# A token-mixing kernel on one core: single row blocks in 64-row halves, one chunk's sums moved, and one step's weight turns re-ordered

## The chip, the cores and the metric

The kernel runs on one NeuronCore of a Trainium2 chip. The time is device microseconds of one execution, the median of several runs. TensorE (PE in the profile) multiplies, VectorE (DVE) and ScalarE (ACT) do elementwise work, GpSimd (POOL) adds and issues DMAs, SyncE (SP) issues DMAs.

## What is computed

Batch 8, sequence 4224, width 192, in two stages. The first is a causal softmax-weighted convolution with 7 taps and one set of weights for each of 8 heads. The second mixes tokens with two dense 4224x4224 matrices:

```python
theta = x @ w_theta
zr, zi = x * np.cos(theta), x * np.sin(theta)
y = np.einsum('ts,bsd->btd', w_tok_r, zr) + np.einsum('ts,bsd->btd', w_tok_i, zi)
u = x + y
out = u + np.maximum(u @ w_ch, 0.0)
```

The two products with 4224x4224 matrices are nearly all of the work.

## The kernel before, in words

**Chunks and blocks.** The tokens that are summed over are cut into 33 chunks of 128 (`NK`), in three groups of 11 (`NW`). The tokens that are written are cut into 33 row blocks of 128 (`NT`), in 17 units: 16 pairs and one single block, the 33rd. The 8 x 192 columns are 1536, seen as two halves of the width (h = 0, 1) of 768 each; a product has 384 moving columns (`BH`), so 768 columns are two products (q = 0, 1).

**Steps.** `Step` t takes one unit (`unit(t)`) and the chunks active at t (`active(t)`; a group's chunks come in over six steps, base 0 to 5, and each stays for 17 steps). There are 58 steps, in order, in rounds of 17: steps 0 to 16 start each unit (`first`), 17 to 40 add to it, 41 to 57 finish it (`final`). The single block has steps 6, 23, 40 and 57, with 11, 11, 9 and 2 chunks. The sums of a unit (`pv`, f32 in SBUF) are loaded from and stored to DRAM (`part`) between rounds.

**Pairs in seven products.** A pair step is a 2x2 product for each chunk: two row blocks (from the two matrices, names "11", "12", "21", "22"; the second digit is the matrix) by two halves of the width (Z11, Z12, Z21, Z22 and differences of them, T1 to T4). It is done in Winograd's form, 7 products in place of 8, with four sums of weights: S1 = 21 + 22, S2 = S1 - 11, S3 = 11 - 21, S4 = 12 - S2. The order of the runs (`runs`, L513) is 11, S1, S2, S4, S3, 12, 22, each over all chunks, with two products (q) a chunk: 154 products in a step of 11 chunks. Each accumulates in a PSUM tile `y` (`ypool`, 2 buffers of two banks): c1 has the runs 11, S2, S3 and 22, c2 S1 and S4, c3 the run 12 in the buffer that c2 leaves. After a run the tile is copied (ScalarE, L496) or added (DVE, L498) into `pv`, and the next run on the same tile waits for that. A single block takes plain products: 4 runs, 88 products of 128x384 with 11 chunks.

**Weights.** `load_w` (L391) loads one matrix's rows for a step as four DMAs from POOL's queue into `st`, of which there are two buffers; a pair has a load of matrix r (m = 1) and one of matrix i (m = 2). `turn` (L404) transposes them 32x32-wise on DVE into a weight tile `wt`, for a pair four turns ("11" and "21" read the first load, "22" and "12" the second), and `wsum` (L416) forms S1 to S4 on DVE. A load can start once the buffer's last turn is done.

**Order.** Each engine's order is written out by hand: `in_order` ties every DVE, PE, ACT and POOL instruction to the one before it. In a step, `mix` issues products and, between them, the events of `step_events(t)`, each with a place from 0 to 7 in units of a seventh of the step. Among the events are the next step's turns and sums (`w_tasks`), the loads for the step after it, and the work on new chunks: convolution (`conv`, L228: 16 products with 96 rows, 64 columns, the two 64-row halves of a PSUM tile in turn), transposes (L174), theta (L150), sine (L303), products (L309) and the differences T1 to T4 (`sums`, L318). The same is done in the front loop (L908) for the first 11 chunks, where a list `LATER` (chunks 8, 9 and 10) has its sums moved into steps 3 and 4. From round 2 on, x is added to `pv` on POOL (`add_x`, L476), with one load buffer `xr` from SP's queue; `paced` ties it to DVE's last instruction at that place.

```python
    LATER = [k for k in range(NW) if start[k] == start[NW - 1]]
    LATER = [LATER[0] - 1] + LATER
```

Of the kernel before, what the change touches and what calls it, by code (L numbers as in the profile page):

```python
# [10 lines left out]
ALU = mybir.AluOpType  # L11
# [5 lines left out]
def kernel(  # L17
# [67 lines left out]
    def pe(ins):  # L85
        return in_order("pe", ins)

    def dve(ins):
        return in_order("dve", ins)
# [261 lines left out]
    class Step:  # L351


        def __init__(self, t):
            self.t, self.u, self.ks = t, unit(t), active(t)
            self.n = len(self.ks)
            self.tbs = [tb for tb in (2 * self.u, 2 * self.u + 1) if tb < NT]
            self.pair = len(self.tbs) == 2
            self.first = t < NU
            self.final = t + NU >= NSTEP  # L360
            self.late = self.final and self.n < NW
            visits = [v for v in range(NU, NSTEP) if v % NU == t % NU]
# [12 lines left out]
            self.plain = self.first and self.pair and self.n <= NP  # L375
            self.time = 0.324 * self.n * (8 if self.plain else 7 if self.pair else 5 if self.n <= 2 else 4)
            self.closing = False
            self.st, self.w, self.xr, self.ub, self.uT, self.pv = {}, {}, {}, {}, {}, []

# [4 lines left out]
        def load_w(self, m):  # L384

            w = (moe_w_tok_r, moe_w_tok_i)[m - 1]
            st = wpool.tile([P, 2, NQ, NW * Q], F16, name="st", tag="st", bufs=2)
            n, nb = self.n * Q, len(self.tbs)
            for a in range(NQ):
                t0 = token(self.ks[0], a)  # L390
                pool(nc.gpsimd.dma_start(  # L391
                    out=st[a * Q : (a + 1) * Q, 0:nb, :, 0:n]
                    .rearrange("i r bt s -> i (r bt) s"),
                    in_=w[self.tbs[0] * P : (self.tbs[0] + nb) * P, t0 : t0 + n]
                    .rearrange("(bt i) s -> i bt s", i=Q),
                ))
            self.st[m] = st
# [4 lines left out]
        def turn(self, name):  # L402
            self.w[name] = self.wtile()
            dve(nc.vector.transpose(  # L404
                self.w[name][:, 0 : self.n, :, :],
                self.st[int(name[1])][:, int(name[0]) - 1, :, 0 : self.n * Q]
                .rearrange("p bt (c j) -> p c bt j", j=Q),
            ))

        def wsum(self, name):  # L410
            a, b, op = {
                "S1": ("21", "22", ALU.add), "S2": ("S1", "11", ALU.subtract),
                "S3": ("11", "21", ALU.subtract), "S4": ("12", "S2", ALU.subtract),
            }[name]
            self.w[name] = self.wtile()
            dve(nc.vector.tensor_tensor(  # L416
                out=self.w[name][:, 0 : self.n, :, :],
                in0=self.w[a][:, 0 : self.n, :, :],
                in1=self.w[b][:, 0 : self.n, :, :], op=op,
            ))  # L420

        def w_tasks(self):

            if not self.pair:
                return [(0.25, lambda: self.turn("11")), (4.2, lambda: self.turn("12"))]
            if self.plain:
                return []
            if self.ahead_of_single():
                return [
                    (0.3, lambda: self.turn("22")), (1.1, lambda: self.wsum("S1")),  # L430
                    (1.9, lambda: self.wsum("S2")), (2.9, lambda: self.turn("12")),
                    (4.0, lambda: self.wsum("S4")),
                ]
            return [
                (0.25, lambda: self.turn("11")), (1.2, lambda: self.turn("21")),
                (2.05, lambda: self.wsum("S3")), (2.2, lambda: self.turn("22")),
                (3.05, lambda: self.wsum("S1")), (3.3, lambda: self.wsum("S2")),
                (4.2, lambda: self.turn("12")), (5.1, lambda: self.wsum("S4")),
            ]

        def ahead_of_single(self):
            return self.final and not steps[self.t - 1].pair and self.pair

        def early_tasks(self):

            return [
                (5.9, lambda: self.turn("11")), (7.0, lambda: self.turn("21")),
                (7.01, lambda: self.wsum("S3")),
            ]
# [110 lines left out]
        def mix_halves(self, events):  # L560
# [31 lines left out]
            for _, f in events:  # L592
                f()

        def mix(self, events):

            if self.n <= 2 and not self.first:
                yield from self.mix_halves(events)
                return
            items = list(self.products())  # L600
            events = sorted(events, key=lambda e: e[0])
            y = {}
            for j, (wn, zn, cn, c, opens, closes, to) in enumerate(items):
                if opens:
                    y[cn] = ypool.tile([P, 2, PC], F32, name="y", tag="y")
                while events and events[0][0] * len(items) <= 7 * j:
                    events.pop(0)[1]()
                k = self.ks[c]
                yield k
                for q in range(2):  # L610
                    pe(nc.tensor.matmul(  # L611
                        y[cn][:, q, 0:BH],
                        lhsT=self.w[wn][:, c, :, :].rearrange("p bt i -> p (bt i)"),
                        rhs=chunks[k].z[:, zn, q * BH : (q + 1) * BH],
                        start=opens, stop=closes,
                        skip_group_check=True,
                    ))
                if to:
                    self.give(y[cn], *to)
            for _, f in events:  # L620
                f()
            if not self.final:
                for i, tb in enumerate(self.tbs):
                    nc.sync.dma_start(
                        out=part[(self.t // NU) % 2][tb, :, :], in_=self.pv[i]
                    )

        def cast_half(self, i, h, gs, by_dve):

# [85 lines left out]
    steps[-2].closing = True  # L715
    NPS = max(s.t for s in steps if s.plain)
    LATER = [k for k in range(NW) if start[k] == start[NW - 1]]
    LATER = [LATER[0] - 1] + LATER
    EARLY = max(k for k in range(NK) if start[k] <= NPS)
    outputs = [  # L720
        (sum(s.time for s in steps[: t + 1]) + at, f)
# [5 lines left out]
    def step_events(t):  # L727
        found = []
        s = steps[t]
        if t + 1 < NSTEP:  # L730
            found += steps[t + 1].w_tasks()
            if not steps[t].ahead_of_single():
                found.append((1.6, steps[t + 1].load_rows))
            for i in steps[t + 1].adds:
                if (t + 1, i) != first_add:
                    found.append((2 + 2 * i, lambda i=i: steps[t + 1].load_x(i)))
                found.append((3.6 + 2 * i, lambda i=i: steps[t + 1].add_x(i)))
        here = [(r, i, which) for r in steps for i, when, which in r.ahead if when == t]
        for j, (r, i, which) in enumerate(here):
            found.append((1.5 + 1.8 * j, lambda r=r, i=i, which=which: r.add_ahead(i, which)))  # L740
        if t + 2 < NSTEP:
            nxt = steps[t + 2]
            if steps[t + 1].ahead_of_single():
                found.append((4.5, lambda: nxt.load_rows(True)))
            for m in (1, 2):
                at = 1.3 + 3 * (m - 1)
                if steps[t + 1].ahead_of_single():
                    at = (0.1, 3.1)[m - 1]
                found.append((at, lambda m=m: nxt.load_w(m)))
            if nxt.ahead_of_single():  # L750
                found += nxt.early_tasks()
        if t == NPS:
            found.append((5.5, lambda: chunks[EARLY].plain_sums()))
        if t == NPS + 1:
# [4 lines left out]
        for j, k in enumerate(LATER):  # L759
            for w in range(2):  # L760
                if start[k] == t + 1:
                    found.append(((2.1 if start[k] == start[NW - 1] else 1.3) + 0.02 * j + 0.01 * w,
                                  lambda k=k, w=w: chunks[k].sums(w)))
        if t == NU - 2:
            def load_wch():
# [230 lines left out]
```

## Time and profile before

| | us |
|---|---|
| runs | 1429.96, 1433.34, 1429.55 (median 1429.96) |
| the profiled execution, its own time | 1430.74 |
| its span, first to last instruction | 1429.0 |
| PE busy | 1409.3 (99%) |
| DVE busy | 973.0 (68%) |
| POOL busy | 437.3 (31%) |
| ACT busy | 312.2 (22%) |

The granted clock of TensorE is 1.000 over the span. In the page and the views a row of a timeline reads: start, length, engine, line, operation, tiles (out<-in), shapes, count, and in brackets the engine's idle time before it with what ended it. Products are pipelined: one is listed with 0.33 us, but they follow each other faster, so a stretch is counted from start to start. Times in the text are from the span's start.

In 40 equal slices of the span TensorE is busy 0.9 or more in all but the first and the last; DVE lies between 0.4 and 0.8.

### The profile page before, as it was taken

The numbers are of one execution on the slowest core, as the hardware profiler recorded it, in microseconds if no ns is written. First come the engines' busy times: TensorE is split into PE (matmuls) and PEld (weight loads), VectorE is DVE, ScalarE is ACT, GpSimd is POOL, SyncE is SP. The second block draws the span as 40 slices with busy tenths as digits, with TensorE's granted clock in tenths as the row PEclk, the third lists the DMA queues.
The fourth block names the chain that finished last, engine by engine and source line by source line (L and its number), as shares of the span: only waits on it lengthen the run. The fifth ranks groups of instructions, "written<-read, shape, count | busy, mean of one in ns | idle before, by whom it ended". The sixth has DMA issues, their size and how long they took to land.

```text
span 1429.0 us, 23779 instructions
## 1 busy us (share of the span) xinstructions
PE 1409.3 (99%) x9829; PEld 889.8 (62%) x9829; DVE 973.0 (68%) x1047; ACT 312.2 (22%) x377; POOL 437.3 (31%) x659
## 2 busy tenths in 40 slices
PE   8999999999999999999999999999999999999998
PEld 5556666666666666666666666666666666666665
DVE  6884554545458787766665657877777677767676
ACT  5951111011134244000000004435200110010134
POOL 8521121111323322532333353333324123213110
PEclk9999999999999999999999999999999999999999
DMA  9985766564699999898899889989999999999884
GB/s 188 244 178 113 152 136 119 111 144 91 158 224 223 238 230 245 207 260 173 231 239 224 236 147 244 239 187 252 278 206 210 216 206 220 202 203 199 162 214 143
DMA packets 272045, 281.99 MB, mean 197 GB/s; under 512 B 106688, under 2 KB 240192, under 8 KB 271936
## 3 DMA queue, kind: packets, MB, share of 16 engines
q0 software_dynamic: 162592, 92.35, 49.2%
q1 hardware_dynamic: 71712, 178.68, 35.5%
q10 hardware_dynamic: 37632, 9.44, 4.6%
q8 instruction: 77, 1.26, 0.4%
q14 instruction: 32, 0.26, 0.1%
HBM read 245.49 MB, written 108.13 MB: 247 GB/s over the span
## 4 chain that ended last, share of the span: by engine, by line
PE 93%; DMA 3%; ACT 1%; DVE 1%; issue 1%; POOL 0%; SPq 0%; DVEq 0%; ACTq 0%
PE y L611 84%; PE v L150 5%; DMA xw<-in_x_dram 2%; PE tp L174 2%; PE pc L228 1%; ACT z L303 1%; DMA part<-pv 0%; DVE pv L498 0%; DMA xs<-z 0%; DMA st<-in_moe_w_tok_i_dram 0%; POOL st L391 0%; ACT uT L160 0%; DVE pv L660 0%; DMA wsb<-in_weight_dram 0%; PE y L576 0%
## 5 line engine op out<-in xcount | busy, mean ns | idle before, releaser
L611 PE MATMUL y<-z,wt 128*128 128x384 f16 x7652 | 1278.0, 326 | 3.4 <-DVE pv L498 2.3
L611 PEld LDWEIGHTS <-wt 128*128 128x128 f16 x7652 | 742.0, 98 | 478.4 <-issue 4.8
L498 DVE TENSOR_TENSOR pv<-y,pv 128x768 f32<-128x768 f32 x315 | 300.8, 955 | 322.0 <-PE y L611 278.9
L404 DVE STREAM_TRANSPOSE wt<-st 128x1408 f16<-128x1408 f16 (+7 forms) x224 | 327.6, 1465 | 43.5 <-PE y L611 36.2
L391 POOL DMA_DIRECT2D st<-in_moe_w_tok_r_dram x232 | 132.6, 578 | 453.4 <-DVE wt L404 445.7
L391 POOL DMA_DIRECT2D st<-in_moe_w_tok_i_dram x232 | 132.6, 578 | 397.9 <-DVE wt L404 386.3
L416 DVE TENSOR_TENSOR wt<-wt 128x1408 f16<-128x1408 f16 (+6 forms) x208 | 173.3, 833 | 41.8 <-PE y L611 39.4
L160 ACT ACTIVATE z<-pc 128x768 f16<-128x768 f32 (+1 forms) x62 | 47.5, 803 | 384.8 <-PE pc L228 380.6
L160 ACT ACTIVATE ub<-pv 128x768 f16<-128x768 f32 (+1 forms) x66 | 51.5, 821 | 338.3 <-DVE pv L498 336.4
L496 ACT ACTIVATE pv<-y 128x768 f32<-128x768 f32 x66 | 53.7, 814 | 278.4 <-PE y L611 278.4
L150 PEld LDWEIGHTS <-uT 128*128 128x128 f16 x1056 | 90.5, 98 | 23.3 <-issue 6.0
L476 POOL TENSOR_TENSOR pv<-pv,xr 128x1536 f32<-128x1536 f32 x24 | 74.5, 3104 | 66.4 <-DVE pv L660 21.9
L208 POOL DMA_DIRECT2D xw<-in_x_dram x132 | 76.4, 585 | 34.1 <-issue 9.2
L660 DVE SCALAR_TENSOR_TENSOR pv<-v,pv 128x768 f32<-128x768 f32 (+1 forms) x67 | 63.0, 942 | 25.2 <-PE v L150 24.7
L318 DVE TENSOR_TENSOR z<-z 128x768 f16<-128x768 f16 x132 | 71.2, 553 | 2.3
L303 ACT ACTIVATE z<-v,half_pi 128x768 f16<-128x768 f32 x66 | 59.7, 904 | 56.4 <-PE v L150 55.7
L160 ACT ACTIVATE uT<-tp 128x1536 f16<-128x1536 f16 (+1 forms) x47 | 56.7, 1209 | 48.8 <-PE tp L174 48.8
L309 DVE TENSOR_TENSOR z<-z 128x1536 f16<-128x1536 f16 (+1 forms) x68 | 60.6, 926 | 4.5 <-ACT z L303 4.5
L150 PE MATMUL v<-wth,uT 128*128 128x192 f16 x528 | 54.4, 246 | 2.7 <-ACT z L303 2.2
L150 PE MATMUL v<-wch,uT 128*128 128x192 f16 x528 | 54.4, 246 | 0.8 <-DVE pv L660 0.5
L303 ACT ACTIVATE z<-v 128x768 f16<-128x768 f32 x66 | 53.2, 807 | 0.0
L228 PE MATMUL pc<-xw,bands 96*64 96x192 f16 x512 | 30.5, 252 | 2.3 <-DMA xw<-in_x_dram 1.6
(49 smaller groups left out, 154.8 us busy)
## 6 DMA issues: line engine op xcount, KB each, us to landing
part<-pv SPq DMA_DIRECT2D x79, 768.0 KB, 4.3
pv<-part SPq DMA_DIRECT2D x79, 768.0 KB, 6.7
out_dram<-pv SPq DMA_DIRECT2D x65, 384.0 KB, 4.5
st<-in_moe_w_tok_r_dram POOLq DMA_DIRECT2D x136, 176.0 KB, 6.0
st<-in_moe_w_tok_i_dram POOLq DMA_DIRECT2D x136, 176.0 KB, 5.3
xs<-z SPq DMA_DIRECT2D x132, 96.0 KB, 5.2
xw<-in_x_dram POOLq DMA_DIRECT2D x121, 96.0 KB, 6.5
xr<-xs SPq DMA_DIRECT2D x24, 384.0 KB, 4.2
```

Source lines behind the costliest of these rows:

```text
L150: pe(nc.tensor.matmul(v[:, k, b * D : (b + 1) * D], lhsT=tT[:, 3 * k + b + i, :], rhs=w[:, 2 * b + i, :], start=(i == 0), stop=(i == 1),))
L160: act(nc.scalar.activation(out=out, in_=in_, func=AT.Copy))
L208: nc.gpsimd.dma_start(out=self.xw[lo : lo + n, h, :, :], in_=x[:, t0 : t0 + n, :].rearrange("b s d -> s b d"),)
L303: act(nc.scalar.activation(**args))
L318: dve(nc.vector.tensor_tensor(out=z[:, o, :], in0=z[:, a, :], in1=z[:, b, :], op=ALU.subtract))
L391: pool(nc.gpsimd.dma_start(out=st[a * Q : (a + 1) * Q, 0:nb, :, 0:n] .rearrange("i r bt s -> i (r bt) s"), in_=w[self.tbs[0] * P : (self.t ...
L404: dve(nc.vector.transpose(self.w[name][:, 0 : self.n, :, :], self.st[int(name[1])][:, int(name[0]) - 1, :, 0 : self.n * Q] .rearrange("p b ...
L416: dve(nc.vector.tensor_tensor(out=self.w[name][:, 0 : self.n, :, :], in0=self.w[a][:, 0 : self.n, :, :], in1=self.w[b][:, 0 : self.n, :, : ...
L476: ins = pool(nc.gpsimd.tensor_tensor(out=self.pv[i], in0=self.pv[i], in1=self.xr[i], op=ALU.add))
L498: dve(nc.vector.tensor_tensor(out=o, in0=yv, in1=o, op=ALU.add))
L611: pe(nc.tensor.matmul(y[cn][:, q, 0:BH], lhsT=self.w[wn][:, c, :, :].rearrange("p bt i -> p (bt i)"), rhs=chunks[k].z[:, zn, q * BH : (q + ...
L660: dve(nc.vector.scalar_tensor_tensor(out=ub[:, ks, :], in0=v[:, ks, :], scalar=0.0, in1=ub[:, ks, :], op0=ALU.max, op1=ALU.add,))
```

## The change

1. `LATER` gets chunk 7 in front of it, so that its four sums leave the front loop; a new place, 0.3, puts the first chunk of the list into step 3 at that place.
2. Steps 6 and 23 (`halves`: single, 11 chunks, not final) cut the single block's 128 rows into two halves of 64 and use the seven products on these. Two products with 64 columns each go side by side, one writing PSUM partitions 0 to 63 and one 64 to 127 of different tiles. The four places are (11 | S1), (S2 | S4), (S3 | 12) and (22 | 22), the last with chunks 0 to 5 beside 6 to 10; each place goes through its chunks with q = 0, then with q = 1, and after each the two halves are emptied into `pv` by DVE (L692), in step 6 the first of each by ScalarE (L690).
3. The two matrices of such a step are loaded into one `st` buffer (`joint`), turned by two turns, and summed by four half-width sums (`half_sums`, L437).
4. The turns, sums and loads of the step behind (7 and 24) get other places: of step 24, turns "11" and "21" go into step 22, "22" and S1 into step 23, S2 and "12" to its end, S4 and S3 into step 24 itself. The loads of the steps around move with the buffers: step 25's second matrix is loaded at the end of step 23, behind turn "12".

```diff
-            self.time = 0.324 * self.n * (8 if self.plain else 7 if self.pair else 5 if self.n <= 2 else 4)
+            self.halves = not self.pair and self.n == NW and not self.final
...
+            joint = self.halves and m == 2
+            if joint:
+                st = self.st[1]
...
+            if self.halves:
+                return [(0.25, lambda: self.turn("11")), (1.2, lambda: self.turn("12")),
+                        (2.2, self.half_sums)]
...
+            if self.behind_halves():
+                if steps[self.t - 1].first:
+                    return [(4.0, lambda: self.wsum("S2")), (7.0, lambda: self.turn("12")),
+                            (7.01, lambda: self.wsum("S4"))]
+                return [(0.0, lambda: self.turn("22")), (0.99, lambda: self.wsum("S1")),
+                        (7.0, lambda: self.wsum("S2")), (7.01, lambda: self.turn("12"))]
...
+            if self.behind_halves() and not steps[self.t - 1].first:
+                return [(3.1, lambda: self.turn("11")), (4.05, lambda: self.turn("21"))]
...
+        def mix_rows(self, events):
+            n = self.n
+            m = (n + 1) // 2
+            every, fore, back = range(n), range(m), range(m, n)
+            slots = [
+                (("11", Z11, every, True, (0, 0)), ("S1", T1, every, True, (1, 1))),
+                (("S2", T2, every, False, (0, 1)), ("S4", Z22, every, False, (0, 1))),
+                (("S3", T3, every, False, (1, 1)), ("12", Z21, every, True, (0, 0))),
+                (("22", T4, fore, False, (1, 0)), ("22", T4, back, True, (1, 0))),
+            ]
...
+                            if opens and c == 0:
+                                y[q, side] = loose("y") if side == 0 else banks("y")
+                            to = slice(64 * side, 64 * side + 64)
+                            pe(nc.tensor.matmul(
+                                y[q, side][to, q, 0:BH],
+                                lhsT=self.half(wn)[:, cs[c], :, :]
+                                .rearrange("p bt i -> p (bt i)"),
+                                rhs=chunks[self.ks[cs[c]]].z[:, zn, q * BH : (q + 1) * BH],
+                                start=opens and c == 0, stop=c == len(cs) - 1,
...
+                        if self.first and (q, i, h) not in copied:
+                            copied.add((q, i, h))
+                            act(nc.scalar.activation(out=o, in_=v, func=AT.Copy))
+                        else:
+                            dve(nc.vector.tensor_tensor(out=o, in0=v, in1=o, op=ALU.add))
...
-    LATER = [LATER[0] - 1] + LATER
+    LATER = [LATER[0] - 2, LATER[0] - 1] + LATER
...
+        if s.behind_halves() and not steps[t - 1].first:
+            found.append((1.0, lambda: s.wsum("S4")))
+            found.append((2.0, lambda: s.wsum("S3")))
...
+                if steps[t + 1].behind_halves() and m == 2:
+                    at = 7.1
...
+                    at = 0.3 if j == 0 else 2.1 if start[k] == start[NW - 1] else 1.3
```

More of the change, by code (lines that the diff above doesn't have):

```diff
@@ L375, in __init__ @@
             self.plain = self.first and self.pair and self.n <= NP
-            self.time = 0.324 * self.n * (8 if self.plain else 7 if self.pair else 5 if self.n <= 2 else 4)
+            self.halves = not self.pair and self.n == NW and not self.final
+            self.time = 0.324 * self.n * (
+                8 if self.plain else 7 if self.pair else 5 if self.n <= 2 else
+                3.55 if self.halves else 4
+            )
             self.closing = False
@@ L386, in load_w @@
             w = (moe_w_tok_r, moe_w_tok_i)[m - 1]
-            st = wpool.tile([P, 2, NQ, NW * Q], F16, name="st", tag="st", bufs=2)
+            joint = self.halves and m == 2
+            if joint:
+                st = self.st[1]
+            else:
+                st = wpool.tile([P, 2, NQ, NW * Q], F16, name="st", tag="st", bufs=2)
             n, nb = self.n * Q, len(self.tbs)
@@ L391, in load_w @@
                 pool(nc.gpsimd.dma_start(
-                    out=st[a * Q : (a + 1) * Q, 0:nb, :, 0:n]
+                    out=st[a * Q : (a + 1) * Q, joint : joint + nb, :, 0:n]
                     .rearrange("i r bt s -> i (r bt) s"),
@@ L405, in turn, with half, half_sums @@
                 self.w[name][:, 0 : self.n, :, :],
-                self.st[int(name[1])][:, int(name[0]) - 1, :, 0 : self.n * Q]
-                .rearrange("p bt (c j) -> p c bt j", j=Q),
-            ))
-        def wsum(self, name):
[L411 to L415, printed above, removed]
+                self.st[int(name[1])][
+                    :, int(name[self.halves]) - 1, :, 0 : self.n * Q
+                ].rearrange("p bt (c j) -> p c bt j", j=Q),
+            ))
+        SUMS = {
+            "S1": ("21", "22", ALU.add), "S2": ("S1", "11", ALU.subtract),
+            "S3": ("11", "21", ALU.subtract), "S4": ("12", "S2", ALU.subtract),
+        }
+        def half(self, name):
+            tile, i = {
+                "11": ("11", 0), "21": ("11", 1), "12": ("12", 0), "22": ("12", 1),
+                "S1": ("S1", 0), "S2": ("S1", 1), "S3": ("S3", 0), "S4": ("S3", 1),
+            }[name]
+            return self.w[tile][:, :, 2 * i : 2 * i + 2, :]
+        def half_sums(self):
+            for name in ("S1", "S2", "S3", "S4"):
+                a, b, op = self.SUMS[name]
+                if name in ("S1", "S3"):
+                    self.w[name] = self.wtile()
+                dve(nc.vector.tensor_tensor(
+                    out=self.half(name), in0=self.half(a), in1=self.half(b), op=op
+                ))
+        def wsum(self, name):
+            a, b, op = self.SUMS[name]
+            if name == "S1" and self.behind_halves() and steps[self.t - 1].first:
+                self.w[name] = self.w[a]
+            else:
+                self.w[name] = self.wtile()
             dve(nc.vector.tensor_tensor(
@@ L442, in ahead_of_single, with behind_halves @@
             return self.final and not steps[self.t - 1].pair and self.pair
+        def behind_halves(self):
+            return self.t > 0 and steps[self.t - 1].halves
         def early_tasks(self):
+            if self.behind_halves() and not steps[self.t - 1].first:
+                return [(3.1, lambda: self.turn("11")), (4.05, lambda: self.turn("21"))]
+            if self.behind_halves():
+                return [
+                    (4.3, lambda: self.turn("11")), (5.2, lambda: self.turn("21")),
+                    (5.3, lambda: self.wsum("S3")), (6.15, lambda: self.turn("22")),
+                    (6.4, lambda: self.wsum("S1")),
+                ]
             return [
@@ L593, in mix_halves @@
                 f()
+        def mix_rows(self, events):
[7 more added lines that the diff above has]
+                (("22", T4, fore, False, (1, 0)), ("22", T4, back, True, (1, 0))),
+            ]
+            total = 2 * sum(len(a[2]) for a, _ in slots)
+            events = sorted(events, key=lambda e: e[0])
+            y, j, copied = {}, 0, set()
+            for slot in slots:
+                for q in range(2):
+                    for c in range(len(slot[0][2])):
+                        while events and events[0][0] * total <= 7 * j:
+                            events.pop(0)[1]()
+                        j += 1
+                        yield self.ks[-1]
+                        for side, (wn, zn, cs, opens, _) in enumerate(slot):
+                            if c >= len(cs):
+                                continue
+                            if opens and c == 0:
[7 more added lines that the diff above has]
+                                start=opens and c == 0, stop=c == len(cs) - 1,
+                                skip_group_check=True,
+                            ))
+                    for side, (_, _, _, _, (i, h)) in enumerate(slot):
+                        o = self.pv[0][64 * i : 64 * i + 64, :].rearrange(
+                            "p (q b h e) -> p q b h e", q=2, h=2, e=HD
+                        )[:, q, :, h, :]
+                        v = y[q, side][64 * side : 64 * side + 64, q, 0:BH].rearrange(
+                            "p (b e) -> p b e", e=HD
+                        )
+                        if self.first and (q, i, h) not in copied:
+                            copied.add((q, i, h))
+                            act(nc.scalar.activation(out=o, in_=v, func=AT.Copy))
+                        else:
+                            dve(nc.vector.tensor_tensor(out=o, in0=v, in1=o, op=ALU.add))
+            for _, f in events:
+                f()
+            self.store_sums()
@@ L595, in mix, with store_sums @@
+        def store_sums(self):
+            for i, tb in enumerate(self.tbs):
+                nc.sync.dma_start(
+                    out=part[(self.t // NU) % 2][tb, :, :], in_=self.pv[i]
+                )
         def mix(self, events):
+            if self.halves:
+                yield from self.mix_rows(events)
+                return
             if self.n <= 2 and not self.first:
@@ L622, in mix @@
             if not self.final:
[L623 to L626, printed above, removed]
+                self.store_sums()
         def cast_half(self, i, h, gs, by_dve):
@@ L730, in step_events @@
         if t + 1 < NSTEP:
-            found += steps[t + 1].w_tasks()
+            least = 1.05 if s.behind_halves() and not steps[t - 1].first else 0
+            found += [(max(at, least), f) for at, f in steps[t + 1].w_tasks()]
             if not steps[t].ahead_of_single():
@@ L748, in step_events @@
                     at = (0.1, 3.1)[m - 1]
+                if nxt.halves:
+                    at = 1.3
+                if nxt.behind_halves():
+                    if m == 1:
+                        continue
+                    at = 2.3
+                if steps[t + 1].behind_halves() and m == 2:
+                    at = 7.1
                 found.append((at, lambda m=m: nxt.load_w(m)))
-            if nxt.ahead_of_single():
+            if nxt.ahead_of_single() or nxt.behind_halves():
                 found += nxt.early_tasks()
+            if nxt.halves:
+                found.append((4.4, lambda: steps[t + 3].load_w(1)))
         if t == NPS:
@@ L761, in step_events @@
                 if start[k] == t + 1:
-                    found.append(((2.1 if start[k] == start[NW - 1] else 1.3) + 0.02 * j + 0.01 * w,
+                    at = 0.3 if j == 0 else 2.1 if start[k] == start[NW - 1] else 1.3
+                    found.append((at + 0.02 * j + 0.01 * w,
                                   lambda k=k, w=w: chunks[k].sums(w)))
```

## The prediction

> **What bounds the kernel now.** I read the page's busy shares and its chain first, then the chain's pieces in order of time, then each engine's timeline where the change lands.
>
> ```profile
> PE 1409.3 (99%) x9829; PEld 889.8 (62%) x9829; DVE 973.0 (68%) x1047; ACT 312.2 (22%) x377; POOL 437.3 (31%) x659
> PE 93%; DMA 3%; ACT 1%; DVE 1%; issue 1%; POOL 0%; SPq 0%; DVEq 0%; ACTq 0%
> ```
> ```profile
> 139.98 272.51 PE y L611 x1677
> ```
>
> TensorE is the chain. The piece from 139.98 us is 1677 products in 272.51 us: **0.1625 us each, no hole**. Steps are found by counting: a pair step of 11 chunks has 154 products (25.02 us), a single block has 88 (14.30 us). By the steps' stretches:
>
> ```profile
> 147.46:161.76 14.30, 14.30 (x90) 8.61 (x89) 7.34 (x7) 2.43 (x3) 4.57 (x8) 1.00 0.94 166
> 568.78:583.08 14.30, 14.30 (x90) 8.61 (x88) 13.07 (x12) 0.00 (x0) 7.21 (x9) 1.00 1.08 295
> 583.08:608.11 25.03, 25.03 (x157) 15.07 (x155) 18.14 (x15) 0.00 (x0) 12.11 (x12) 1.00 0.83 171
> ```
>
> These are steps 6, 23 and 24 (columns: length, PE, PEld, DVE, ACT, POOL, granted clock, DMA, GB/s). PE is full at clock 1.00, so a product saved counts whole. But DVE is already busy 13.07 of 14.30 us in step 23: that is where a change can put TensorE behind DVE.
>
> **Part 1, chunk 7's four sums** (L318, 2.2 us together) go from the end of the front loop into step 3. TensorE has one hole there:
>
> ```profile
> 74.63 0.82 PE L150 MATMUL v<-wth,uT 128*128 128x192 f16 x8 [0.16 <-ACT z L303]
> 77.03 0.48 PE L611 MATMUL y<-z,wt 128*128 128x384 f16 x2 [1.58 <-DVE pv L498]
> ```
>
> The L498 that it waits for stood behind those sums on DVE. With them gone TensorE goes on at 75.29, **1.74 us earlier**. Then step 3, DVE:
>
> ```profile
> 81.89 1.37 DVE L404 STREAM_TRANSPOSE wt<-st 128x1152 f16<-128x1152 f16 x1
> 85.55 1.83 DVE L309 TENSOR_TENSOR z<-z 128x1536 f16<-128x1536 f16 x2 [2.29 <-ACT z L303]
> ...
> 96.41 0.95 DVE L498 TENSOR_TENSOR pv<-y,pv 128x768 f32<-128x768 f32 x1
> ```
>
> DVE idles 2.29 us and then works almost without a hole to the L498 that ends at 97.36. The bank that it empties is opened next at item 70 of step 3, at 97.41: DVE already sets this moment, to 0.05 us. In the changed kernel (I read the order in which its built instructions stand on each engine) the sums stand behind the first L309, which still waits for ScalarE (now 1.74 earlier, at 83.8). From there: 0.95 + 2.2 of sums + the same work as before, and L498 ends at 97.35. TensorE comes to it 1.74 early and **gives it all back**. I take 0; the ends are 0 and -1.74.
>
> **Part 2, TensorE in steps 6 and 23.** 88 products become 154 of 64 columns, in 11 + 11 + 11 + 6 = 39 places for each of two column halves: 78 places, 76 of 2 and 2 of 1. No row has such a product with 128 rows and 384 columns. The nearest is the convolution, two 64-column halves side by side:
>
> ```profile
> 411.68 0.81 PE L611 MATMUL y<-z,wt 128*128 128x384 f16 x4
> 412.43 0.85 PE L228 MATMUL pc<-xw,bands 96*64 96x192 f16 x16
> 413.21 3.10 PE L611 MATMUL y<-z,wt 128*128 128x384 f16 x18
> ```
>
> Sixteen of 192 take 0.85 us; eight lone ones (L150, above) take 0.82. In the instruction list the second of a pair starts 3 to 4 ns after the first and pairs follow at 82.5 ns. So a pair costs a lone one's time. Ends: 0.1625 (its stream of 384 cannot be shorter) and 0.325; I take **0.1625**. Going in costs 412.43 - 412.17 - 0.16 = 0.09 us, coming out 0.10. A step is 78 x 0.1625 + 0.19 = 12.87, **1.43 less**.
>
> **Part 3, emptying the banks.** Each run's half now is emptied by two operations of 64x384 (L692 of the changed kernel): 16 in all, against 3 of 0.955. Ends: 0.40 and 0.955; nearest row:
>
> ```profile
> L588 DVE TENSOR_TENSOR pv<-y,pv 128x384 f32<-128x384 f32 x4 | 2.2, 554 | 0.3 <-PE y L576 0.3
> ```
>
> I take 0.554, 0.47 where two follow each other (rows overlap by 0.08). DVE starts 0.37 us after the last product's start (568.62 to 568.99). A group of 11 places lasts 1.79 us and two empties 1.0, so most hide. The group of 6 lasts 0.975: the fourth run's second half opens a bank (7 places, 1.14 us, after the last start) that is empty only at 0.37 + 0.47 + 0.55 + 0.05 = 1.44. **0.3 us of stall in each step**; step 23 loses 0.05 more where a 1.64 us turn stands ahead of the first empties. Net: -1.12 and -1.07. At 0.955 an empty, it would be +1 us a step more.
>
> The half sums (704 elements; L416 of 768 takes 0.551) fall into idle DVE in step 5 and into 551.1 to 554.6 in step 22. At double price the next L498 comes 0.9 late, before its bank is wanted: nothing.
>
> **Part 4, the new order in steps 7 and 21 to 25.** By DVE's order, step 24's first two turns move into step 22 (the turn of step 23's second matrix, which stood there, is earlier too), its third to the head of step 23. DVE leaves step 22 at the same moment as before. Step 7: the early banks are emptied by ScalarE and no POOL add is about; a load of 704 KB issued at 163.5 would have to take over 10.7 us to hurt, while that round's rows have 6.6 to 8.6 in all. Nothing.
>
> Step 24 is the one that I fear. Its last turn (second matrix, "12") now comes after step 23's empties, and only it frees the buffer into which step 25's second matrix is loaded. The POOL queue before that load holds the second add (L476). Before, the same load was issued at 581.2:
>
> ```profile
> 578.15 3.11 POOL L476 TENSOR_TENSOR pv<-pv,xr 128x1536 f32<-128x1536 f32 x1 [2.55 <-DVE wt L416]
> 581.20 2.31 POOL L391 DMA_DIRECT2D st<-in_moe_w_tok_i_dram  x4
> 585.64 3.10 POOL L476 TENSOR_TENSOR pv<-pv,xr 128x1536 f32<-128x1536 f32 x1 [2.13 <-issue]
> ```
>
> Laid end to end: step 23 ends at 582.0; empties end at 583.1. The first add starts behind the sixth empty, 575.6 to 578.7; xr's transfer takes 3 to 3.8 us; the second add runs at about 582.1 to 585.2, or, if DVE's sum (S2) gets in first, 584 to 587.1. A sum that meets an add waits for it:
>
> ```profile
> 601.10 3.10 POOL L476 TENSOR_TENSOR pv<-pv,xr 128x1536 f32<-128x1536 f32 x1 [9.05 <-DMA xr<-xs]
> ```
> ```profile
> 602.03 2.92 DVE L416 TENSOR_TENSOR wt<-wt 128x1408 f16<-128x1408 f16 x1
> ```
>
> 2.92 in place of 0.88, ending 0.75 after the add. The Trainium skill, "SBUF — State Buffer", section "SBUF: two separate sides", has it that whichever of the two starts first keeps a shared port for its whole instruction; the trace agrees on DVE waiting (2.92 us), and no run here shows POOL waiting. Either way the sum and turn "12" end at 585.5 to 587.6, and the load goes out at **587.1 to 587.6**. Its four transfers go out within 1.73 us; the slowest takes, after 581.2, 604 and 625.4:
>
> ```profile
> DMA to landing us min/median/max: 4.6/6.2/7.3
> ```
> ```profile
> DMA to landing us min/median/max: 4.2/6.9/11.3
> ```
> ```profile
> DMA to landing us min/median/max: 3.9/5.4/5.9
> ```
>
> So 7.6 to 13.0 us in all; beside an xr load and a part store, as here, 9.0 and 13.0, with the store ahead 7 to 8.5. I take 8.5: landed at 596.1. DVE runs in order, and turn "22" of step 25, which waits for it, stands ahead of the L498 that empties S2's run. S3's run wants that bank at 582.0 + 88 x 0.1625 = 596.3; turn and L498 take 1.64 + 0.95 - 0.08 + 0.05, so the load would have to be there at 593.75. **Stall 2.4, say 2.5 us** (0 to 7). After it nothing is late: DVE has 0.9 us of room at the next bank.
>
> **Sum.** The profiled execution took 1430.74 us, span 1429.0 and 1.74 around it. Span: 1429.0 - 1.12 - 1.07 + 2.5 = 1429.3; time 1431.0. The median of the runs is 0.78 below the profiled one: **1430.3 us**.
>
> **The rivals.**
> (a) The load of step 25 comes in time: no stall, -2.2, 1427.8. It decides at 6.6 us; for it, the load of 814.9 took 6.4 in all. Against: one transfer ran beside that one; here there are two or three.
> (b) Besides, step 3 keeps its 1.74: 1426.1, and 0.6 less if the short group does not stall. Against: L498's 0.05 us.
> (c) Load slow (13 us) and issued behind a later add: stall over 6.5, 1434.5 to 1436.
> (d) **Slower**: pairs run one after the other. 76 x 0.1625 x 2 = +24.7, and the stalls of 3.1 hide under it: 1451.9. It decides from a second product that starts 0.16 us after the first, not 4 ns; the convolution speaks against it.
> (e) A pair costs a quarter more than a lone one: +6.3, 1436.6; slower over 0.3% from about a sixth. Against: 0.85 to 0.82 above. The Trainium skill, "TensorE: Matmul & The Clock Gate", section "Measured speedup vs the span model", has three column tiles at 2.38 times one, so 1.26 of a lone product's time; an estimate by it is 0.205 us a pair and 1436.9 us.
>
> **Chances.** Forecast (stall 0.5 to 6.4) 0.66; (a) 0.14; (b) 0.08; (c) 0.06; (d) 0.03; (e) 0.03. About 0.3% (4.3 us) is what a measurement of this kernel can tell from no change. Faster by more: half of (b), 0.04. Slower: (c), (d), (e), 0.12. Within: 0.84. The range 1426.5 to 1434.5 leaves out half of (b) and (c) to (e), 0.16.
>
> **What would show it.** Steps 6 and 23: 13.2 us each, 154 products of 128*64 in pairs, two waits of 0.3 us on L692. The wait of 1.58 at 77 gone, one of 1.7 near 95.7, the first on the L498 of now, the second on the same operation, L549 of the changed kernel. In step 24 one TensorE wait of 2 to 3 us on L549, behind a DVE turn that waits for the second matrix's load. I am wrong in the pairs if the steps last over 14.3, and in step 24 if that turn waits for nothing.

## The result, and the profile after

The changed kernel takes 1434.08 us (median of 22 runs, 1429.1 to 1442.9) beside 1430.26 us for the kernel before on the same chips (22 runs, 1428.45 to 1439.14): ratio 1.0023, 95% interval 1.0013 to 1.0033, so 2 to 5 us slower. The profiled execution took 1435.94 us, its span is 1434.2 us. In the profiles of both kernels TensorE also waits for loads of x for the convolution (xw), longer in one execution than in another; the steps' lengths below keep that apart.

The waits of TensorE (line waited for: us in total, times, longest), after:

```profile
PE y L722 <- DVE pv L549: 6.3, 5, 3.6
...
PE pc L228 <- DMA xw<-in_x_dram: 1.7, 1, 1.7
```

Before, the first was 2.3 us in 3 waits, the longest 1.6. So there is 4 us more of waiting for an emptying by DVE. Where? Counted by products, as in the prediction, steps 6, 23 and 24 of the changed kernel are these stretches (columns: length, busy us of PE, PEld, DVE, ACT, POOL, granted clock, DMA, GB/s):

```profile
150.16:163.24 13.08, 12.99 (x155) 8.76 (x155) 4.70 (x8) 4.20 (x8) 0.00 (x0) 1.00 0.51 148
570.37:583.73 13.36, 13.18 (x156) 10.10 (x155) 10.98 (x18) 0.00 (x0) 3.11 (x1) 1.00 0.74 268
583.73:614.70 30.97, 27.04 (x157) 15.57 (x156) 22.05 (x21) 0.00 (x0) 16.15 (x15) 0.94 0.79 164
```

Steps 6 and 23 became 1.22 and 0.94 shorter. Step 24 went from 25.03 to 30.97, **5.94 us longer**, and its granted clock is 0.94. Step 2 is 1.76 shorter and step 3 1.82 longer. Together: -1.22 - 0.94 + 5.94 + 0.06 = +3.8 us. The other 1.4 us of the span's 5.2 lie in stretches whose instructions did not change. Step 1 is the largest of them: 2.43 longer, by a wait for xw and by a stretch at half clock (below); against it stand shorter ones (step 0 by 0.57, step 38 by 0.47).

Step 24, DVE and then TensorE:

```profile
585.12 2.53 DVE L447 TENSOR_TENSOR wt<-wt 128x1408 f16<-128x1408 f16 x1
587.57 1.63 DVE L412 STREAM_TRANSPOSE wt<-st 128x1408 f16<-128x1408 f16 x1
...
599.75 1.65 DVE L412 STREAM_TRANSPOSE wt<-st 128x1408 f16<-128x1408 f16 x1 [3.12 <-DMA st<-in_moe_w_tok_i_dram]
601.32 0.92 DVE L549 TENSOR_TENSOR pv<-y,pv 128x768 f32<-128x768 f32 x1
```
```profile
594.97 3.73 PE L722 MATMUL y<-z,wt 128*128 128x384 f16 x22 [0.34 <-DVE pv L549]
602.29 4.93 PE L722 MATMUL y<-z,wt 128*128 128x384 f16 x19 [3.59 <-DVE pv L549]
```

The sum S2 (585.12) takes 2.53 us because POOL's add runs to 586.90; the turn "12" behind it ends at 589.2, and POOL can issue the load only then:

```profile
583.80 3.10 POOL L527 TENSOR_TENSOR pv<-pv,xr 128x1536 f32<-128x1536 f32 x1 [3.25 <-DMA xr<-xs]
589.50 2.30 POOL L399 DMA_DIRECT2D st<-in_moe_w_tok_i_dram  x4 [2.60 <-DVE wt L412]
```

Its last transfer lands 8.4 us after its own issue (591.22), at 599.63. The turn "22", ahead of the emptying in DVE's order, waits 3.12 us for it, and TensorE waits 3.59 us for the emptying. That is not the end: here is the same stretch in slices of 3.41 us, and others for comparison.

```profile
40.26:43.67 3.41, 1.31 (x13) 0.72 (x12) 3.38 (x5) 0.85 (x2) 2.10 (x5) 1.00 1.49 257
43.67:47.08 3.41, 3.41 (x22) 2.15 (x20) 0.09 (x1) 1.96 (x4) 1.68 (x3) 0.50 1.23 318
98.28:101.70 3.42, 1.75 (x12) 1.05 (x12) 3.38 (x4) 0.00 (x0) 0.17 (x1) 1.00 0.00 0
600.04:603.46 3.42, 1.17 (x8) 0.71 (x8) 3.32 (x4) 0.00 (x0) 0.00 (x0) 1.00 0.96 138
603.46:606.87 3.41, 3.41 (x12) 1.55 (x11) 2.99 (x3) 0.00 (x0) 2.76 (x1) 0.50 0.01 1
```

In the slice that starts 1.2 us after the wait, TensorE gets **half its clock**: 12 rows where 21 products fit, each 0.32 us instead of 0.1625. A slice at half clock costs half of 3.41, 1.7 us. So step 24's 5.94 is 3.6 (the wait) + 0.35 (a wait ahead of it) + 1.7 (the clock) and 0.3 of smaller pieces. In the front two waits near each other, the longer for xw, did the same at 43.67; the wait of 1.67 us in step 3, in the slice from 98.28, did not.

### The profile page after: what moved, and what is told of

Read it like the earlier page. It is cut to its first block, busy times and chain, and to the rows that moved or that the text cites. A ratio compares the mean times of both kernels' runs of the same rounds, so it can differ in the third digit from the quotient of the medians.

```text
span 1434.2 us, 24086 instructions
## 1 busy us (share of the span) xinstructions
PE 1410.8 (98%) x9961; PEld 893.0 (62%) x9961; DVE 985.4 (69%) x1075; ACT 314.1 (22%) x383; POOL 436.3 (30%) x659
## 4 chain that ended last, share of the span: by engine, by line
PE 91%; DVE 3%; DMA 3%; ACT 1%; issue 1%; POOL 1%; SPq 0%; DVEq 0%; POOLq 0%; ACTq 0%
PE y L722 81%; PE v L150 5%; PE tp L174 2%; PE pc L228 1%; PE y L673 1%; ACT z L303 1%; DMA xw<-in_x_dram 1%; DVE wt L412 1%; DMA st<-in_moe_w_tok_i_dram 1%; POOL st L399 0%; DVE pv L692 0%; DMA part<-pv 0%; DVE wt L447 0%; DMA pv<-part 0%; DMA st<-in_moe_w_tok_r_dram 0%
## 5 line engine op out<-in xcount | busy, mean ns | idle before, releaser
L722 PE MATMUL y<-z,wt 128*128 128x384 f16 x7476 | 1252.6, 326 | 7.4 <-DVE pv L549 6.3
L722 PEld LDWEIGHTS <-wt 128*128 128x128 f16 x7476 | 725.1, 98 | 473.2 <-issue 10.2
L549 DVE TENSOR_TENSOR pv<-y,pv 128x768 f32<-128x768 f32 x311 | 297.0, 955 | 296.7 <-PE y L722 264.9
```

The source lines that it names most:

```text
L549: dve(nc.vector.tensor_tensor(out=o, in0=yv, in1=o, op=ALU.add))
L722: pe(nc.tensor.matmul(y[cn][:, q, 0:BH], lhsT=self.w[wn][:, c, :, :].rearrange("p bt i -> p (bt i)"), rhs=chunks[k].z[:, zn, q * BH : (q + ...
```

## Experiments

Each was compared with the kernel before on its chip (medians 1430.3 to 1430.8). A gain of 1 us is below what a ratio tells here (intervals of about 0.15% each way), so single steps are judged by their length in the profile.

**turn_late: is it DVE's order in step 24?**

```diff
+            if self.t > 1 and steps[self.t - 2].halves and not steps[self.t - 2].first:
+                return [
+                    (0.25, lambda: self.turn("11")), (1.2, lambda: self.turn("21")),
+                    (2.05, lambda: self.wsum("S3")), (4.02, lambda: self.turn("22")),
+                    (4.03, lambda: self.wsum("S1")), (4.04, lambda: self.wsum("S2")),
+                    (4.2, lambda: self.turn("12")), (5.1, lambda: self.wsum("S4")),
+                ]
```

> The changed kernel, but the turn of step 25's second matrix ("22"), which waits for that matrix's load, stands behind the emptying of S4's run in step 24 instead of ahead of the emptying of S2's run. Theory (the long wait in step 24 is the load seen through DVE's order): the wait of 3.6 us on the emptying goes, the products after it run at full clock, step 24 lasts 25.0 to 25.4 us (a wait of 0.34 us, for the emptying of S1's run, stays), and the whole is 1430.3 - 1.2 - 0.95 + 0.35 = about 1428.5, 5 to 6 us below the changed kernel. Rival 1 (the load itself is too late for whatever needs it): the wait moves to the first products that need the sum S1, in step 25, and the time stays at 1433 to 1435. Rival 2 (the cost lies in the pairs or in the front, not in step 24): no change, 1434.

Measured: 1429.21 us (12 runs), ratio 0.9995 (0.998 to 1.001), about 5 us below the changed kernel. Step 24:

```profile
583.68:609.21 25.53, 25.20 (x156) 15.08 (x155) 21.97 (x21) 0.00 (x0) 15.07 (x15) 1.00 0.88 167
```

25.53 in place of 30.97, clock 1.00. The load was issued at 589.45, 5.77 us into the step as in the changed kernel, and its last transfer landed at 599.43: as late as ever, and nobody waited for it on TensorE's side. Step 25 is as long as before. Rivals 1 and 2 fall: the load is late only for a turn that stands ahead of an emptying.

The profiled execution of this run shows the clock elsewhere. In step 18 TensorE waits 2.81 us for xw, nearly all of it within one slice, and the next slice is at half clock; step 18 is 4.62 us longer than in the kernel before:

```profile
442.44:445.85 3.41, 0.72 (x5) 0.20 (x2) 3.11 (x3) 0.00 (x0) 2.40 (x5) 1.00 1.05 316
445.85:449.26 3.41, 3.29 (x21) 2.02 (x22) 0.00 (x0) 1.51 (x2) 1.47 (x3) 0.50 1.15 313
```

**halves_one and halves_two: the pairs in one step alone**

```diff
-            self.halves = not self.pair and self.n == NW and not self.final
+            self.halves = not self.pair and self.n == NW and not self.final and self.first
```

(halves_two has `and not self.first`; both leave chunk 7's sums as before.)

> The kernel before with the pairs of 64-column products in step 6 alone, and the new order that this brings to steps 4 to 8; chunk 7's sums where they were, steps 22 to 25 as before. Theory: step 6 lasts 13.1 in place of 14.3 us and nothing else moves: 1.2 below the kernel before, 1429.0. Rival (the new order of step 7 costs as that of step 24 does): a wait in step 7 or 8, 1431 or more.

> The kernel before with the pairs in step 23 alone, and the new order of steps 22 to 25; step 6 and chunk 7's sums as before. Theory (step 24's wait comes from this part): step 23 0.95 shorter, step 24 longer by 4.0 where the clock stays and by 5.9 where it falls after the wait; 3 to 5 above the kernel before, 1433 to 1435. Rival (the wait comes from elsewhere, the front or step 6): 1429.3.

Measured: halves_one 1429.22 us, ratio 0.9998 (0.9984 to 1.0013); by time alone this can't be told from the kernel before. By the profile step 6 lasts 13.08 us, and steps 7 and 8 are within 0.15 us of the kernel before: nothing is paid behind step 6. halves_two 1435.80 us, ratio 1.0032 (1.0015 to 1.0049): the loss is in this part. In its profiled execution the load's four transfers landed sooner (8.4 us from first issue to last landing, against 10.1), and TensorE's wait was half as long:

```profile
598.98 6.33 PE L722 MATMUL y<-z,wt 128*128 128x384 f16 x38 [1.86 <-DVE pv L549]
```

The slice that held most of the wait had TensorE busy 1.54 us, and the clock stayed behind it:

```profile
596.84:600.25 3.41, 1.54 (x10) 0.83 (x9) 3.31 (x4) 0.00 (x0) 0.00 (x0) 1.00 1.34 202
600.25:603.67 3.42, 3.42 (x23) 2.05 (x21) 3.42 (x4) 0.00 (x0) 2.87 (x1) 1.00 0.20 31
```

Step 24 lasted 27.59 us, +2.56. So the same order in step 24 loses 2.6 us in one execution and 6 in another.

**after_again: the changed kernel once more** (no edit)

> The changed kernel once more, for a second look at its step 24 and at how its time scatters. Theory: the wait on the emptying is 1.9 to 3.6 us, as the load's landing makes it; where it is over 3 us the clock halves for 3.4 us behind it and the run is 5 to 6 us longer than in runs where it is about 2; median 1433 to 1435. Rival (the time of the changed kernel is set by the front): step 24 the same each time, and the runs differ in steps 1 and 18.

Measured: 1433.65 us, ratio 1.0019 (1.0008 to 1.0029). In its profile the wait is 3.7 us and step 24 lasts 31.13 (+6.11):

```profile
579.14:610.27 31.13, 27.03 (x156) 15.65 (x155) 22.06 (x21) 0.00 (x0) 16.12 (x15) 0.95 0.78 161
```

Of the three profiles with this order two had the long wait and the halved clock, one the short wait. In all 34 runs of the changed kernel those (7) with mean clock 1.000 took 1429.1 to 1430.9 us, those (16) with 0.997 or less 1431.6 to 1442.9. The 11 between, at 0.998 and 0.999, run from 1429.8 to 1438.9, so the clock alone does not set the time. One halved slice in 1434 us lowers the mean by 0.0012. The front adds to that scatter too (the changed kernel's first profile lost a slice there), so the share of step 24 in it is not separated run by run.

**swap: does the load's issue set the wait?**

```diff
-                        (7.0, lambda: self.wsum("S2")), (7.01, lambda: self.turn("12"))]
+                        (7.0, lambda: self.turn("12")), (7.01, lambda: self.wsum("S2"))]
```

> The changed kernel with one swap in step 24: the turn "12" of its second matrix ahead of the sum S2 on DVE, instead of behind it. The sum waits for POOL's second add (2.53 us in place of 0.88); a turn beside an add took its usual 1.64 us. Theory (the stall of step 24 is the chain add, sum, turn, load, turn, emptying): the turn ends before the add does, the load goes out right behind the add, 2.5 us earlier, and the wait on the emptying shrinks from 1.9 to 3.6 us to 0 to 1.2 us; step 24 at most 26.6 us, time 1430 or less, clock falling seldom. Rival (the load's landing is set by the other transfers, not by its issue): it lands at the same moment, wait as before, 1434.

Measured: 1428.59 us, ratio 0.9992 (0.9975 to 1.0009). POOL, DVE and TensorE:

```profile
583.99 3.10 POOL L527 TENSOR_TENSOR pv<-pv,xr 128x1536 f32<-128x1536 f32 x1 [3.24 <-DMA xr<-xs]
587.28 2.31 POOL L399 DMA_DIRECT2D st<-in_moe_w_tok_i_dram  x4 [0.18 <-issue]
```
```profile
585.33 1.65 DVE L412 STREAM_TRANSPOSE wt<-st 128x1408 f16<-128x1408 f16 x1
586.90 0.94 DVE L447 TENSOR_TENSOR wt<-wt 128x1408 f16<-128x1408 f16 x1
```
```profile
599.32 6.01 PE L722 MATMUL y<-z,wt 128*128 128x384 f16 x36 [0.91 <-DVE pv L549]
```

The turn ran beside POOL's add in its usual 1.65 us, and the sum, now behind the add, in 0.94 in place of 2.53. The load goes out 3.35 us into the step instead of 5.77, the wait is 0.91, step 24 lasts 26.11 us, and the wait of 0.34 us is gone too. Two places exchanged take back most of the loss. The load's last transfer lands at 596.65, 12.7 us into the step instead of 15.9, so its issue does set the landing, and the rival falls. (In the front this profile lost a slice to the clock, behind a wait of 2.22 us for xw.)

**sums_alone: part 1, placed elsewhere, on the kernel before**

```diff
-    LATER = [LATER[0] - 1] + LATER
+    LATER = [LATER[0] - 2, LATER[0] - 1] + LATER
...
+                    at = 6.2 if j == 0 else 2.1 if start[k] == start[NW - 1] else 1.3
```

> The kernel before with one edit: chunk 7's four sums behind the last emptying of step 3 instead of at the end of the front loop. Theory: step 2 1.76 us shorter, step 3 as before, 1.7 below the kernel before: 1428.5 to 1429. Rival (what stands in step 3 waits for ScalarE or for DVE anyway): the wait comes back in step 3 or 4, no change.

Measured: 1428.64 us, ratio 0.9989 (0.9976 to 1.0001); in the profile step 2 is 1.59 shorter and step 3 as long as before. With the place 0.3 of the change step 3 took it back in all four profiles that had it (+1.82 or +1.83):

```profile
90.70 7.64 PE L722 MATMUL y<-z,wt 128*128 128x384 f16 x46
100.01 16.26 PE L722 MATMUL y<-z,wt 128*128 128x384 f16 x99 [1.67 <-DVE pv L549]
```

(the changed kernel; in sums_alone this row runs through, 87.66 to 106.20 without a wait). The gain was real, and was lost to the place that the sums were given.

**turn_sums_late, best_two, best_three: the mends together**

turn_sums_late is turn_late with the place 6.2 for the sums. best_two also moves step 25's turn "21" from 1.2 to 2.03, best_three its turn "12" from 4.2 to 5.03, each behind an emptying:

```diff
-                    (0.25, lambda: self.turn("11")), (1.2, lambda: self.turn("21")),
+                    (0.25, lambda: self.turn("11")), (2.03, lambda: self.turn("21")),
...
-                    (4.2, lambda: self.turn("12")), (5.1, lambda: self.wsum("S4")),
+                    (5.03, lambda: self.turn("12")), (5.1, lambda: self.wsum("S4")),
```

> As turn_late, and chunk 7's four sums go behind the last emptying of step 3 instead of its head, so that DVE reaches the emptying on which TensorE waits in step 3 without them. Theory (the front's gain was given back because the sums, 2.2 us of DVE, were put in the same chain again): TensorE keeps the 1.74 us, no wait of 1.7 in step 3, 1428.5 - 1.7 = 1426.8. Rival 1 (the gain is given back elsewhere, at the emptying of step 4 that then comes 1 us late, or by ScalarE): as turn_late, 1428.5. Rival 2 (the sums are then too late for step 4's second run): a wait in step 4, 1429 or more.

> As turn_sums_late, and in step 24 the turn "21" of step 25 behind the emptying of S1's run instead of ahead of it. Theory (the wait of 0.34 us there was that turn): step 24 25.03 us, 0.45 below turn_sums_late; against the kernel before -1.76 - 1.22 - 0.94 = -3.9 us, 1426.5, ratio 0.9973. Rival (the turn now pushes a later emptying past its time): a wait of 0.3 to 1 us at the next bank, no gain on turn_sums_late.

> As best_two, and the turn "12" of step 25 behind the emptying of S3's run instead of ahead of it. Theory (the wait of 0.33 us that best_two showed in step 24 was this turn): step 24 25.03 us, no wait; against the kernel before -1.76 - 1.22 - 0.94 = -3.9 us, 1426.5 to 1427. Rival (the turn now holds up the emptying of the next run): a wait of 0.3 us or more at the end of step 24 or the head of step 25, as best_two.

Measured: turn_sums_late 1428.53 us, ratio 0.9985 (0.9969 to 1.0); best_two 1427.06 us, 0.9978 (0.9963 to 0.9994); best_three 1428.91 us, 0.9987 (0.9971 to 1.0003). In best_two the wait of 0.34 us only moved, from the emptying of S1's run to that of S3's (0.33 us, turn "12" ahead of it), as the rival had it. In best_three step 24 has none:

```profile
581.34:606.37 25.03, 25.03 (x156) 15.08 (x155) 22.66 (x21) 0.00 (x0) 13.69 (x15) 1.00 0.78 161
```

Its profiled execution lost 2.4 us in steps 18 and 22 to xw instead. By the steps' lengths best_three should be 3.9 below the kernel before and best_two 3.4; the three ratios say 2 to 3, and do not tell the three from each other. best_two is faster than both kernels; best_three is faster than the changed one, and by its time not clearly faster than the one before. The medians expected for turn_sums_late and best_three, 1426.8 and 1426.5 to 1427, were missed by about 2 us.

**stalls: what does a wait cost?** The kernel before with work added; `again` repeats the turn into the tile that it has just filled:

```diff
+            for i in range({26: 3, 27: 4, 28: 3, 29: 4, 30: 3, 31: 4, 32: 2, 33: 5}.get(t, 0)):
+                found.append((2.85 + 0.001 * i, lambda: steps[t + 1].again("22")))
```

> The kernel before with DVE work added that changes no result: in steps 26 to 33 the turn "22" is repeated 3, 4, 3, 4, 3, 4, 2 and 5 times ahead of the emptying of S2's run. By that emptying's slack of 2.63 us and 1.58 us a repeat TensorE waits 2.1, 3.7, 2.1, 3.7, 2.1, 3.7, 0.5 and 5.3 us, 23.2 us in all. Theory (a long wait costs 1.7 us on top of its length, since the clock halves for 3.4 us afterwards; it falls where a slice of 3.4 us that TensorE's own clock gate cuts freely was idle for over about two thirds): after 5.3 always, after 3.7 mostly, after 2.1 seldom or never, after 0.5 never; 1430.5 + 23.2 + 3 to 5 times 1.7 = 1459 to 1462. Rival (a wait costs its length): 1453.7.

Measured: 1465.50 us (4 runs). The holes between products and what the steps lost:

| repeats | hole beyond 0.16 us | step longer by |
|---|---|---|
| 2 (step 32) | 0.67 | 0.67 |
| 3 (26, 28, 30) | 2.30, 2.35, 2.30 | 2.29, 2.35, 2.29 |
| 4 (27, 29, 31) | 3.97, 4.03, 3.98 | 5.56, 5.62, 5.63 |
| 5 (step 33) | 5.71 | 7.33 |

Here a wait of up to 2.35 us costs its length, and one from 3.97 on costs 1.6 more, each time. But the six waits of 3 and 4 repeats tell less than six: steps 26, 28 and 30 begin 58 us apart, which is 17 slices of 3.413 us, and so do 27, 29 and 31. Like waits therefore fall alike across the slices. Each wait of 2.3 us lay 0.6 to 0.7 us in one slice and the rest in the next. Steps 26 and 27:

```profile
649.38:652.79 3.41, 1.54 (x10) 0.95 (x10) 3.31 (x4) 0.00 (x0) 0.00 (x0) 1.00 0.01 2
676.68:680.10 3.42, 0.00 (x0) 0.00 (x0) 3.39 (x3) 0.00 (x0) 0.00 (x0) 1.00 0.46 111
680.10:683.51 3.41, 3.26 (x11) 1.53 (x11) 3.31 (x5) 0.00 (x0) 0.00 (x0) 0.50 0.00 0
```

The holes themselves were 0.2 to 0.4 longer than expected. The eight steps lost 31.7 us; the median rose by 35. In the profile step 42 is 5.45 us longer too (a wait of 3.6 us for a transpose by DMA, and a slice at half clock behind it), and step 1 is 2.3 longer; whether they are so in every run stays open.

## Why the prediction was right, and where it was short

The time lies inside the range, 0.4 us below its upper end, and 3.8 us above the forecast of 1430.3. That it lies inside is in part luck: the upper end was set for a stall by the load alone, and it happened to hold the loss by the clock, which the prediction did not have.

- **What bounds the kernel:** right. All that moved the time is TensorE's products saved or TensorE waiting.
- **Part 1:** right. It came 1.76 earlier to step 3 (1.74 expected) and gave back 1.82 on the emptying named, at 98.2 to 100.0. sums_alone shows that the place was the cause.
- **Part 2:** right. In the changed kernel's instruction list pairs follow each other at 0.1625 us, and entering and leaving cost about 0.1 each; 78 x 0.1625 + 0.2 + one wait of 0.26 = 13.1, measured 13.08. Rival (e) is out. The figure for three column tiles in the Trainium skill, "TensorE: Matmul & The Clock Gate", section "Measured speedup vs the span model", is no guide to two here: 1.26 of a lone product's time would have made step 6 16.3 us (an estimate: 13.08 and 76 x 0.0425).
- **Part 3:** right in kind. One emptying takes 0.51 to 0.56 us (0.554 taken); the wait at the short group is 0.26 (0.3). Step 23 has a second wait of 0.25 where 0.05 was expected, behind the turn of 1.64 us and a sum of 0.89 on DVE. Net -1.22 and -0.94 against -1.12 and -1.07.
- **Part 4, step 7:** right (halves_one).
- **Part 4, step 24: the step that was short.** The chain was the one described, link for link: add, sum held up beside it, turn, load, turn "22", emptying of S2's run. Issue came 5.77 us into the step (5.1 to 5.6 expected), the load took 10.1 us and in after_again 10.3 (8.5 taken, 13 the far end), and the wait was 3.6 to 3.7 us where "Stall 2.4, say 2.5 us" stood; in halves_two, with a load of 8.4 us, it was 1.86. So the load was taken 1.6 to 1.8 us too short, and two terms were put at nothing, without a reason. Before the big wait TensorE waits 0.34 us for the emptying of S1's run, behind two turns. And behind a wait that fills most of a slice the clock halves, which costs 1.7 us more. The sum should have had 3.6 + 0.35 + 1.7 + 0.3 = 5.9 in place of 2.5, with 2.6 in the good case: 1430.3 + 3.4 = 1433.7.
- **Rivals:** (c) had the right order, a stall worth 6.5 us or more and 1434.5 to 1436, for a partly other reason: the load was not 13 us, the rest was the clock. (a) did not happen in any of the three profiles with this order, nor did (b) or (d).

With a load of 10.1 us and the clock among the terms, the forecast would have been 1433.7 us, close to (c), a case at 0.06. The waits between products that the trace of before showed, at most 1.6 us, could not tell the clock's part.

## What to carry to other kernels

In an in-order queue, place a work item that waits for a load behind the copies that free TensorE's banks, not ahead of them; and put the op that frees a load's buffer ahead of one that will be held up beside another engine's work. Price a wait of TensorE at its length, and at 1.7 us more if it can fill over half of one slice of 3.41 us. All waits between products of 3.6 us and more here did; of the waits of 1.6 to 2.8 us some did (2.81, 2.22, 1.88 in halves_one and, with another beside it, 1.67 us, all for xw) and some did not (1.67 in step 3, 1.86 in halves_two, 2.30 to 2.35 in stalls). What decided, as far as the traces show it, is how much of one slice was idle in all. Work moved off one critical place is a gain only if it does not land ahead of the next one in the same queue.

## What the runs showed of the hardware

**The clock falls by slices of 3.41 us, and a slice need not be idle for it.** In the changed kernel's trace the two halved slices start at 43.67 and 603.46 us, 559.8 us apart, 164 times 3.413. The slice before each had TensorE busy 1.31 and 1.17 of 3.41 us (38% and 34%). In all twelve traces, behind the first 12 us, every slice with TensorE busy at most 40% was followed by one at half clock, and none with 49% or more was. Between them it went both ways: behind 1.54 us (45%) the clock halved in the front of halves_one and stayed in step 24 of halves_two; why is open. So a wait over two slices may pass unpunished (2.30 to 2.35 us in stalls), and a shorter one that falls into one slice is punished (2.22 us in swap's front, with 1.17 us busy). The Trainium skill, "TensorE: Matmul & The Clock Gate", section "Part 1: The HAM clock gate", has a free-running window of about 3.4 us and the half rate; the traces agree on both (0.50 granted in each of the slices above). It says that the clock drops after an idle window; here 38% busy was still too little, and the measurement decides.

**A sum waits for POOL's add, a turn does not.** Beside the same add the f16 sum took 2.53 us, behind it 0.94, while the 128x1408 turn beside it took 1.65 us (swap), as it does elsewhere. The Trainium skill, "SBUF — State Buffer", section "SBUF: two separate sides", has it that a DVE operation with two SBUF inputs competes with such an add for a shared port; the trace agrees, for the sum has two and the turn one.
